# Order on ScalarE and VectorE in a routed expert kernel: casts and conversions keep their place, evictions and router steps rank higher

## The chip, the cores and the metric

The kernel runs on one core of one Trainium2 chip. The metric is the device time of one execution in microseconds (us). Its engines, each with an instruction order of its own, are TensorE (PE for its matmuls, PEld for its weight loads), VectorE (DVE), ScalarE (ACT), GpSimd (POOL) and SyncE (SP), which issues most DMAs.

## What is computed

Three stages follow one another: attention with a memory term gives 2304 tokens of 512 values; a router assigns each token to one of 8 experts with 288 places each, strictly in the order of the scores, and each expert is a pair of matrices with a relu between; a last pair of matrices has a gate between.

```python
a = softmax(causal(q @ k.T / 8));  x = g * mem_out + (1 - g) * (a @ v)     # 4 x 8 heads, 576 x 64
logits = x @ w_gate                                                        # 2304 x 8
for idx in np.argsort(-logits.flatten()):                                  # best pair first
    tok, e = idx // 8, idx % 8
    if assigned[tok] >= 0 or counts[e] >= 288: continue
    assigned[tok] = e; counts[e] += 1
y[mask_e] = np.maximum(x[mask_e] @ w1[e], 0) @ w2[e]                       # 512 -> 1024 -> 512
h = y @ w_in                                                               # 512 -> 2048, w_in is float64
out = (h * np.tanh(np.log1p(np.exp(h)))) @ w_out                           # 2048 -> 512, float64 weights
```

## The kernel before

**Stages.** `attention` fills the DRAM tensor xd (tokens) and the tile L (scores). Then `moe` does all the rest, one expert of 288 tokens at a time. Every product is made of three matmuls of 128 x 128 weights with 288 tokens (`mm3`, L1011), since both sides are held as a rounded part and a remainder; the second part of a tile is always the first's difference.

**The program of `moe`.** A list `plan` names the matmul items: `up` and `down` of the expert (pass 1), then the first half (pass 2) and second half (pass 3) of the gated pair. All pass 3 items come last, when nothing else is left to prepare. One item is usually 12 matmuls. Around the items run generators, called processes: the router (`routing`), loads of weights (`loads`), their casts (`splits`), conversions of the float64 weights (`conversions`), the gathers of tokens (`tokens`), the gates (`gate`) and the evictions of results (`relu`, `both`, `to_o`, `to_part`). `slot()` lets each process take one step; an item calls it about twice, and a process that yields n sits out n slots. A process has a class, which is its order within a slot: EVAC 0, ROUTE 1, GATE 1.5, TURN 2, LOAD 3, CONV 4.

**What sets the order on an engine.** TensorE and GpSimd issue in the order in which the program is written (`manual_schedule`, X["MO"]). ScalarE, VectorE and SyncE are ordered by a planner that simulates time: when an engine is free in its simulation, the ready operation with the best rank goes, and the rank is the place in the program, shifted by `tc.high_priority(offset=...)` (a positive offset is earlier). `tc.issue_after(ins)` adds an order edge: what the block writes on that instruction's engine is issued behind it. On the chip the order found is fixed; an operation whose input is late holds up all that stand behind it on its engine.

**Weights of the experts.** Of each expert 16 tiles are used in pass 1, 128 in all. `loads` (L921) brings one into one of five raw buffers (RAWB), once the router knows the expert (L908 reads its number). `splits` waits until LD slots after the load, then casts it on ScalarE (L942), writes its negative (L944), and lets a DMA of GpSimd add the raw value to that (L950), which leaves the remainder; once the router is done, VectorE subtracts instead (L953). Seven results are held (WFB). A raw buffer is free when the accumulation has read it. The casts have rank -400.

**Conversions.** Sixteen tiles of w_in and w_out are converted from float64 during `moe`: the load (L766, L769) and the store (L796) are issued by GpSimd; between them stand the mask (L779, VectorE), the scaling (L780, ScalarE) and five VectorE operations (L782 to L793). Sixteen others are converted during attention with SyncE as the queue. Pass 3 reads the results (`raw<-w`).

**Router.** `Router.phase` finds an expert's 288 tokens: six search steps, each a compare on VectorE (cm, L710), 18 small matmuls (L715), two short VectorE steps (ge L725, ind L727), one matmul (L730); then counts (L608, bt L634, L637) and the tokens' places (ohp L671, gc L665, L676, idx L681).

**Evictions and gates.** `relu` writes act (ScalarE L1052, VectorE L1054). `both` writes xt and y (L1002, L1004). `gate` takes sigmoid, copy, arctan and sine on ScalarE (L1076 to L1085; sines in groups of four) and four VectorE operations (L1089 to L1092).

Of the kernel before, what the change touches and what calls it, by code (L numbers as in the profile page):

```python
# [11 lines left out]
AF = mybir.ActivationFunctionType  # L12
OP = mybir.AluOpType
# [9 lines left out]
LA, LC, LD, AHEAD = 3, 0, 2, 6  # L23
# [10 lines left out]
def attention(tc, ctx, q, k, v, M_prev, z_prev, beta, w_gate, xd, L, side=None):  # L34
# [250 lines left out]
    def stage_a(u, i):  # L285
# [34 lines left out]
        if hs is None:  # L320
            nc.vector.tensor_reduce(nm, sb[:, :, 0:w], axis=AX.X, op=OP.max, negate=True)
        else:
            nc.vector.tensor_reduce(nm[:, hs:hs + 1], vw[hs][:, 0:w], axis=AX.X, op=OP.max, negate=True)  # L323
        for h in heads:
# [50 lines left out]
    def stage_d(u, i):  # L375
# [21 lines left out]
        if hp == NP - 1:  # L397
# [3 lines left out]
            nc.vector.tensor_reduce(L[d0:d0 + n, j, :], xa[d0:d0 + n, :, D:W].rearrange("p h e -> p e h"),  # L401
                                    axis=AX.X, op=OP.add)

# [141 lines left out]
class Router:  # L545
# [18 lines left out]
    def wait(self, i):  # L564
        return WAIT[2 if self.done <= self.cur + X["AH"] else self.busy][i]

# [7 lines left out]
    def phase(self, k):  # L574
# [5 lines left out]
        with self.after():  # L580
            nc.vector.tensor_reduce(m, L, axis=AX.X, op=OP.max)

# [6 lines left out]
        mx = rp.tile([128, NJ], F32, name="mx")  # L589
        nc.vector.tensor_reduce(mx, w, axis=AX.X, op=OP.max)  # L590
        oh = rp.tile([128, NJ, E], BF, name="oh")
# [158 lines left out]
LEAST, MOST = (struct.unpack("f", struct.pack("i", e << 20))[0] for e in (896, 1151))  # L750


def converter(tc, w_in, w_out):


    nc = tc.nc
    U16 = dt.uint16
    w32 = nc.dram_tensor("w32", [2, 16, 128, 512], F32, kind="Internal").ap()
    whl = nc.dram_tensor("whl", [2, 8, 128, 2, 512], F32, kind="Internal").ap()

    def convert(a, f, cv, raw, parts=None, eng=nc.gpsimd, queue=nc.sync):


        def load():
            if a == 0:
                queue.dma_start(raw.bitcast(U16).rearrange("p (a f) w -> p a (f w)", a=4),  # L766
                                w_in.bitcast(U16)[:, f * 512:(f + 1) * 512].rearrange("(a p) f -> p a f", p=128))
            else:
                queue.dma_start(raw.bitcast(U16).rearrange("p f w -> p (f w)"),  # L769
                                w_out.bitcast(U16)[f * 128:(f + 1) * 128, :])  # L770

        load()
        yield 10
        hi = raw[:, :, 1]
        t = cv.tile([128, 512], I32, name="cvt")
        e = cv.tile([128, 512], U16, name="cve")
        r = cv.tile([128, 512], F32, name="cvr")

        nc.vector.tensor_scalar(t, hi, 0x7FFFFFFF, None, op0=OP.bitwise_and)  # L779
        nc.scalar.activation(r, raw.bitcast(U16)[:, :, 1], AF.Copy, scale=2.0 ** -36)  # L780
        yield
        nc.vector.tensor_scalar(t.bitcast(F32), t.bitcast(F32), LEAST, MOST, op0=OP.max, op1=OP.min)  # L782
        yield

        nc.vector.tensor_scalar(t, t, 5, 2, op0=OP.logical_shift_left, op1=OP.logical_shift_right)
        nc.vector.scalar_tensor_tensor(t, hi, -0x40000000, t, op0=OP.bitwise_and, op1=OP.bitwise_or)
        yield

        nc.vector.tensor_scalar(e, t.bitcast(U16).rearrange("p (f w) -> p f w", w=2)[:, :, 1], 0xFF80, None,
                                op0=OP.bitwise_and)  # L790
        eng.tensor_mul(r, r, e.bitcast(BF))
        yield
        eng.tensor_add(r, r, t.bitcast(F32))  # L793
        if parts is None:
            yield 4
            queue.dma_start(w32[a, f], r)  # L796
            return
        yield
        parts = parts()
        nc.scalar.copy(parts[:, 0], r)  # L800
        nc.gpsimd.tensor_sub(parts[:, 1], r, parts[:, 0])
        nc.sync.dma_start(whl[a, f], parts.bitcast(F32))

    return convert, w32, whl


def moe(tc, ctx, C, xd, L, w1, w2, w32, whl, convert, out):
    nc = tc.nc
# [30 lines left out]
    def slot():  # L839
        for p in list(procs):  # L840
            if p[0] == hold[0]:
                continue
            p[1] -= 1
            if p[1] <= 0:
                try:
                    p[1] = next(p[2]) or 1
                except StopIteration:
                    procs.remove(p)

    def until(cond):  # L850
        while not cond():
            slot()

    EVAC, GATE, ROUTE, TURN, LOAD, CONV = X["CL"]


    def woven(ups, downs, rate):
# [76 lines left out]
    def splits():  # L934
        for c, n, key in order:
            while not flight or flight[0][4] + X["LD"] > count[0] or n - used[c] >= cap[c]:
                yield 1
            t = flight[0][3]
            dst = (fp if c == "wf" else wp).tile([128, 2, 512], F32R, name=c, bufs=cap[c])

            with tc.high_priority(offset=-400):
                nc.scalar.copy(dst[:, 0], t)  # L942
                if R.done < E:
                    nc.scalar.activation(dst[:, 1], t, AF.Copy, scale=-1.0)  # L944
            yield 1
            if R.done < E:

                while turned[0] < -1:
                    yield 1
                nc.gpsimd.dma_start(dst[:, 1].bitcast(F32), t, accum_op=OP.add)  # L950
            else:

                nc.vector.tensor_sub(dst[:, 1], t, dst[:, 0])  # L953
            flight.pop(0)
            ready[c, key] = dst
            yield 1
# [57 lines left out]
    def up(w, x, then):  # L1014

        p = hbank()
        for d in range(ND):
            mm3(p[:, 0:CAP], w, d, lambda b, d=d: x[:, b, d, :], d == 0, d == ND - 1)
            if d == 1:
                slot()  # L1020
        h = Act(fp.tile([128, 2, CAP], F32R, name="act", bufs=X["ACTB"]))
        spawn(then(h, p), GATE if then is gate else EVAC)
        return h
# [92 lines left out]
    spawn(routing(), ROUTE)  # L1116
    spawn(loads(), LOAD)
    spawn(splits(), LOAD)
    spawn(conversions(), CONV)
    for k in range(E):  # L1120
# [85 lines left out]
    for u, c, k, f in plan:  # L1206
# [26 lines left out]
    until(lambda: len(scat) == G * E)  # L1233


X = {"MO": ("PE", "Pool"), "P": 4, "P0": 4, "L1": 2, "RX": 0, "XB": 2, "LAG": 6, "TW": 18, "TS": 2, "LD": 6,
     "LG": 2, "RAWB": 5, "WFB": 7, "ACTB": 12, "GB": 7, "NG": 4, "CL": (0, 1.5, 1, 2, 3, 4), "C0": 2,
     "CW": 4, "FW": 3, "FE": 4, "AH": 2}


def program(tc, q, k, v, M_prev, z_prev, beta, w_gate, w1, w2, w_in, w_out, out):
# [54 lines left out]
```

## Time and profile before

| | us |
|---|---|
| median of three runs | 1127.38 (1124.45 to 1130.71) |
| the profiled execution | 1125.07 |
| its span, first to last instruction | 1123.2 |
| busy in the span: PE, PEld | 1009.8, 932.5 |
| busy in the span: ACT, DVE, POOL | 681.1, 652.2, 343.7 |

The profile is one execution, taken by the hardware. A line of a timeline has the start in us from the span's beginning, the duration, the engine, the line of the code, the operation, the tiles (out<-in), their shapes, the count, and in brackets how long the engine had been idle and what ended that. SPq and POOLq are the sequencers of SyncE and GpSimd. "PEclk" is the granted clock of TensorE as a share of 2.4 GHz. A wait for several things is put down to the one that came last.

### The profile page before, as it was taken

The page shows a single profiled execution, that of the slowest core. Times are in us where ns is not written, and L with a number is a line of the kernel's source. Part 1 is how long each engine was busy: PE and PEld are TensorE (multiplying, and loading weights), DVE is VectorE, ACT ScalarE, POOL GpSimd, SP SyncE. Part 2 cuts the span into 40 slices and gives each one's busy share as a digit, 9 for nine tenths or more (in the row PEclk, how much of TensorE's full clock was granted, in tenths as well). Part 3 has the DMA queues.
Part 4 walks back from the last instruction along what each step waited for, and adds up shares of the span by engine and source line. Part 5 has one row for each costly group of instructions (what it writes and reads, how often), then busy time and mean ns, then how long its engine had stood idle before and what let it go on. Part 6 is the DMA issues. An engine that isn't in the chain of part 4 may idle for free. (4 is left out here: it accounts for less than half of the span.)

```text
span 1123.2 us, 22421 instructions
## 1 busy us (share of the span) xinstructions
PE 1009.8 (90%) x8088; PEld 932.5 (83%) x8088; DVE 652.2 (58%) x1986; ACT 681.1 (61%) x1632; POOL 343.7 (31%) x468
## 2 busy tenths in 40 slices
PE   5999899999837879889789999799999999999995
PEld 4778778788726868779679888799999999999995
DVE  7877777876663565576476585566443533333332
ACT  5677676767404483564465655647483986666662
POOL 5677566674204131403304333220000001111112
PEclk9999899999957988899899999999999999999998
DMA  7899969896199685937929948755435412222201
GB/s 179 212 231 242 230 183 231 215 239 158 42 347 197 149 218 134 237 99 169 250 79 219 249 135 207 197 156 165 137 119 164 157 73 85 86 85 85 75 22 43
DMA packets 177488, 182.61 MB, mean 163 GB/s; under 512 B 90912, under 2 KB 131904, under 8 KB 175328
## 3 DMA queue, kind: packets, MB, share of 16 engines
q1 hardware_dynamic: 157152, 134.59, 41.6%
q0 software_dynamic: 20224, 46.58, 19.3%
q8 instruction: 64, 1.05, 0.4%
q14 instruction: 48, 0.39, 0.1%
HBM read 97.17 MB, written 36.18 MB: 119 GB/s over the span
## 5 line engine op out<-in xcount | busy, mean ns | idle before, releaser
L1011 PE MATMUL acc<-act,wb 128*128 128x288 f32 x1536 | 234.8, 303 | 3.1 <-ACT o L1153 1.4
L1011 PEld LDWEIGHTS acc<-act,wb 128*128 128x128 f32 x1536 | 216.5, 193 | 5.3 <-DVE act L1092 2.2
L950 POOL DMA_DIRECT2D wf<-raw x93 | 83.6, 967 | 254.9 <-ACT wf L944 184.6
L1089 DVE TENSOR_TENSOR H<-H,U 128x288 f32<-128x288 f32 x128 | 56.8, 455 | 172.3 <-ACT U L1085 172.3
L942 ACT CAST wf<-raw 128x512 fp32r<-128x512 f32 x128 | 78.7, 617 | 95.3 <-DMA raw<-moe_w 75.8
L1011 PE MATMUL h<-xt,wf 128*128 128x288 f32 x768 | 125.3, 309 | 5.4 <-DVE xt L1004 3.6
L1011 PE MATMUL h<-y,wa 128*128 128x288 f32 x768 | 119.7, 310 | 5.8 <-ACT y L1002 3.7
L1178 POOL DMA_INDIRECT out<-xg,idx x24 | 24.3, 1011 | 326.7 <-ACT xg L1175 326.1
L1011 PE MATMUL acc<-act,wf 128*128 128x288 f32 x768 | 121.1, 308 | 3.1 <-ACT act L1052 3.1
L1011 PEld LDWEIGHTS h<-xt,wf 128*128 128x128 f32 x768 | 110.5, 196 | 10.7 <-DVE xt L1004 4.6
L1011 PEld LDWEIGHTS h<-y,wa 128*128 128x128 f32 x768 | 109.5, 197 | 11.4 <-issue 3.9
L1011 PEld LDWEIGHTS acc<-act,wf 128*128 128x128 f32 x768 | 109.5, 196 | 5.3 <-ACT act L1052 3.2
L1011 PE MATMUL h<-xt,wa 128*128 128x288 f32 x768 | 113.1, 296 | 0.0
L1011 PEld LDWEIGHTS h<-xt,wa 128*128 128x128 f32 x768 | 105.2, 188 | 0.0
L1076 ACT ACTIVATE U<-h 128x288 f32<-128x288 f32 x128 | 53.1, 415 | 84.0 <-PE h L1011 83.1
L342 ACT COPY T<-pt 128x512 f32<-128x512 f32 (+3 forms) x128 | 57.7, 455 | 63.5 <-PE pt L341 63.0
L325 ACT ACTIVATE P<-s,nm 128x576 f32<-128x576 f32 (+4 forms) x160 | 84.2, 535 | 6.7 <-DVE nm L323 5.9
L1052 ACT ACTIVATE act<-h 128x288 fp32r<-128x288 f32 x64 | 25.9, 405 | 91.5 <-PE h L1011 91.3
L341 PE MATMUL pt<-ident,P 128*128 128x128 f32 x400 | 71.0, 285 | 0.5 <-DVE T L342 0.3
L367 PE MATMUL o<-T,vm 128*64 128x128 f32 x640 | 64.2, 288 | 0.0
L1054 DVE SCALAR_TENSOR_TENSOR act<-h,act 128x288 fp32r<-128x288 f32 x64 | 29.1, 454 | 60.2 <-ACT act L1052 59.9
L309 PE MATMUL s<-k,q 128*128 128x288 f32 (+3 forms) x192 | 60.0, 349 | 0.3 <-ACT P L325 0.2
(237 smaller groups left out, 2060.7 us busy)
## 6 DMA issues: line engine op xcount, KB each, us to landing
raw<-moe_w SPq DMA_DIRECT2D x128, 256.0 KB, 4.0
wf<-raw POOLq DMA_DIRECT2D x93, 256.0 KB, 4.9
k<-kh SPq DMA_DIRECT2D x60, 160.0 KB, 3.8
yd<-y SPq DMA_DIRECT2D x8, 1152.0 KB, 5.7
xt<-yd SPq DMA_DIRECT2D x8, 1152.0 KB, 5.7
whl<-parts SPq DMA_DIRECT2D x16, 512.0 KB, 5.4
part<-o SPq DMA_DIRECT2D x8, 576.0 KB, 3.4
wf<-part SPq DMA_DIRECT2D x16, 288.0 KB, 3.2
```

The source lines that it names most:

```text
L309: nc.tensor.matmul(vw[h][:, a:e], q1[:, h, r], k1[:, h, kb[h] + a:kb[h] + e], start=True, stop=False, skip_group_check=True)
L325: nc.scalar.activation(P[:, h * w:(h + 1) * w], vw[h][:, 0:w], AF.Exp, bias=nm[:, h:h + 1], scale=1.0, accum_out=den[:, h:h + 1])
L341: nc.tensor.transpose(t[:, j * 128:(j + 1) * 128], P[:, (c + j) * 128:(c + j + 1) * 128], ident)
L342: (nc.scalar.copy if eng else nc.vector.tensor_copy)(T[:, c:c + m], t[:, 0:m * 128].rearrange("p (a b) -> p a b", b=128))
L367: nc.tensor.matmul(o[s, 0:n], vm[:, j - 1 if h else 4 - j, h, :], T[:, i + j if h else i - j, 0:n], start=False, stop=(j == i), skip_group ...
L942: nc.scalar.copy(dst[:, 0], t)
L950: nc.gpsimd.dma_start(dst[:, 1].bitcast(F32), t, accum_op=OP.add)
L1011: nc.tensor.matmul(p, w[:, a, c * 128:(c + 1) * 128], x(b), start=first and i == 0, stop=last and i == 2)
L1052: nc.scalar.activation(h.t[:, 0], p[:, 0:CAP], AF.Relu)
L1054: nc.vector.scalar_tensor_tensor(h.t[:, 1], p[:, 0:CAP], 0.0, h.t[:, 0], op0=OP.max, op1=OP.subtract)
L1076: s = nc.scalar.activation(U, p[:, 0:CAP], AF.Sigmoid, scale=-1.0)
L1089: nc.vector.tensor_mul(H, H, U)
```

## The change

A helper `placed(tc, eng)` gives an order edge behind the last instruction written so far on an engine. The casts of weights use it (L942, L944), and so do a conversion's mask and scaling where its queue is GpSimd's. There the step after the load comes 14 slots later in place of 10. Each step of a process is written under a rank shift by class: +300 for evictions and router, -600 for conversions, 0 for others; the casts keep -400. LD goes from 6 to 8 and the pause between conversions, CW, from 4 to 2.

```diff
+def placed(tc, eng):
+
+    return tc.issue_after(next(i for i in reversed(tc.nc.cur_bb.bb.instructions) if i.engine == eng.engine))
...
         load()
-        yield 10
+        yield 10 if queue is nc.sync else 14
...
-        nc.vector.tensor_scalar(t, hi, 0x7FFFFFFF, None, op0=OP.bitwise_and)
-        nc.scalar.activation(r, raw.bitcast(U16)[:, :, 1], AF.Copy, scale=2.0 ** -36)
+        with nullcontext() if queue is nc.sync else placed(tc, nc.vector):
+            nc.vector.tensor_scalar(t, hi, 0x7FFFFFFF, None, op0=OP.bitwise_and)
+        with nullcontext() if queue is nc.sync else placed(tc, nc.scalar):
+            nc.scalar.activation(r, raw.bitcast(U16)[:, :, 1], AF.Copy, scale=2.0 ** -36)
...
-                    p[1] = next(p[2]) or 1
+                    with tc.high_priority(offset=AHEAD.get(p[0], 0)):
+                        p[1] = next(p[2]) or 1
...
+    AHEAD = {EVAC: X["PE"], ROUTE: X["PR"], CONV: -X["PC"]}
...
-            with tc.high_priority(offset=-400):
+            with placed(tc, nc.scalar), tc.high_priority(offset=-400):
...
-X = {"MO": ("PE", "Pool"), "P": 4, "P0": 4, "L1": 2, "RX": 0, "XB": 2, "LAG": 6, "TW": 18, "TS": 2, "LD": 6,
+X = {"MO": ("PE", "Pool"), "P": 4, "P0": 4, "L1": 2, "RX": 0, "XB": 2, "LAG": 6, "TW": 18, "TS": 2, "LD": 8,
      "LG": 2, "RAWB": 5, "WFB": 7, "ACTB": 12, "GB": 7, "NG": 4, "CL": (0, 1.5, 1, 2, 3, 4), "C0": 2,
-     "CW": 4, "FW": 3, "FE": 4, "AH": 2}
+     "CW": 2, "FW": 3, "FE": 4, "AH": 2, "PE": 300, "PR": 300, "PC": 600}
```

## Rows read from the trace of the kernel before

**Rows 1.** The page's head and part 1: busy us, share of the span, instructions.
```profile
span 1123.2 us, 22421 instructions
...
PE 1009.8 (90%) x8088; PEld 932.5 (83%) x8088; DVE 652.2 (58%) x1986; ACT 681.1 (61%) x1632; POOL 343.7 (31%) x468
```

**Rows 2.** Windows by stage: length, each engine's busy us, clock, DMA share, GB/s.
```profile
344.00:756.00 412.00, 360.07 (x2973) 337.04 (x2974) 247.09 (x861) 230.89 (x488) 124.04 (x141) 0.93 0.73 181
756.00:1100.00 344.00, 341.52 (x2566) 339.81 (x2566) 144.54 (x367) 235.18 (x505) 21.97 (x40) 1.00 0.32 103
```

**Rows 3.** Windows at clock 0.50 behind gaps of A (4), B (4), C (3): sums.
```profile
sum 23.89, PE 16.68 PEld 15.71 DVE 13.95 ACT 18.67 POOL 14.81; mean PE 4.17 PEld 3.93 DVE 3.49 ACT 4.67 POOL 3.70
...
sum 13.64, PE 13.18 PEld 12.26 DVE 7.46 ACT 6.58 POOL 3.00; mean PE 3.29 PEld 3.06 DVE 1.86 ACT 1.64 POOL 0.75
...
sum 17.06, PE 16.23 PEld 14.40 DVE 16.14 ACT 5.18 POOL 2.37; mean PE 5.41 PEld 4.80 DVE 5.38 ACT 1.73 POOL 0.79
```

**Rows 4.** PE's waits, 344 to 756: waiter, releaser, total us, times, longest us.
```profile
PE rt L715 <- DVE cm L710: 11.8, 4, 7.9
PE rt L730 <- DVE ind L727: 7.4, 4, 3.6
PE rt L637 <- DVE bt L634: 7.2, 2, 5.2
...
PE h L1011 <- ACT y L1002: 3.7, 1, 3.7
PE h L1011 <- DVE xt L1004: 3.6, 2, 3.0
PE acc L1011 <- ACT act L1052: 3.1, 1, 3.1
PE rt L715 <- DVE oh L592: 2.3, 1, 2.3
...
PE h L1011 <- ACT xt L1002: 1.7, 1, 1.7
```

**Rows 5.** ACT's waits, 344 to 756.
```profile
ACT wf L942 <- DMA raw<-moe_w: 41.6, 22, 8.3
```

**Rows 6.** Timeline around 550: a cast on ACT, and PE's end of waiting.
```profile
547.97 0.62 ACT L942 CAST wf<-raw 128x512 fp32r<-128x512 f32 x1 [8.33 <-DMA raw<-moe_w]
...
552.27 0.64 PE L715 MATMUL rt<-oh,cm 128*32 128x8 bf16 x18 [7.90 <-DVE cm L710]
```

**Rows 7.** Timeline of DVE, 694 to 698: conversion steps between router steps.
```profile
695.51 0.41 DVE L785 TENSOR_SCALAR cvt<-cvt 128x512 int32<-128x512 int32 x1
...
696.36 0.68 DVE L786 SCALAR_TENSOR_TENSOR cvt<-raw,cvt 128x512 int32<-128x512 int32 x1
696.96 0.44 DVE L634 TENSOR_REDUCE bt<-q 128x36 bf16<-128x288 bf16 x1
```

**Rows 8.** Timeline around 498: the gate's sines on ACT and the copies of xt.
```profile
496.56 1.81 ACT L1085 ACTIVATE U<-U,half_pi 128x288 f32<-128x288 f32 x4
...
498.28 0.97 ACT L1002 CAST xt<-h 128x288 fp32r<-128x288 f32 x3
```

**Rows 9.** Timeline of SP, 340 to 372: loads of the first expert's weights.
```profile
344.05 24.24 SPq L921 DMA_DIRECT2D raw<-moe_w  x11
```

**Rows 10.** Chain that ended last: start, us, one item of 12 matmuls at full clock.
```profile
1093.36 1.60 PE h L1011 x12
```

**Rows 11.** Instructions of L950 (accumulation): duration ns min/median/max, first and last start.
```profile
L950 POOL DMA_DIRECT2D wf<-raw x93: 841/857/2279, 340.2 to 742.0; - x93
...
DMA to landing us min/median/max: 3.3/4.9/7.8
```

**Rows 12.** Instructions of L921 (loads of weights), in the same form.
```profile
L921 SPq DMA_DIRECT2D raw<-w x16: 319/320/332, 845.6 to 897.4; - x16
...
DMA to landing us min/median/max: 2.4/3.8/8.0
```

**Rows 13.** Instructions of L769 (conversion's load of w_out), in the same form.
```profile
L769 POOL DMA_DIRECT2D raw<-moe_w_out x8: 554/857/1597, 409.4 to 747.7; - x8
```

## What the change will do to the time

> **What bounds the kernel now.** First the page's head: one core, a span of 1123.2 us, TensorE busy 90% of it [rows 1]. An average of 90% says little, so next the busy time by stage [rows 2]. Attention ends at 307, the router's first pass at 344. From 344 to 756 the experts are chosen and their weights prepared: TensorE is busy 360 of 412 us at a mean clock of 0.93. From 756 to 1100 it is busy 341.5 of 344 us at full clock: nothing is to be had there. The last 23 us are transposes and scatters; these, attention and the first pass the change hardly touches. So the question is what the change does to the 52 us in which TensorE stands still between 344 and 756, and to the clock there.
>
> Third view: TensorE's waits in that stretch [rows 4]. Its order is written out by hand, so a late operand of the next matmul stops everything behind it. The waits look scattered; following each back along the engine that released it gives three classes, 40.8 us of the 52.
> - A, a weight cast at the head of ScalarE. At 547.97 a cast starts after 8.33 us of waiting for its load; behind it stand the output copies (L1002), behind their subtraction on VectorE a compare of the router (cm), and TensorE starts again at 552.27 [rows 6]. The longest waits for cm, for ind, for y and for act are of this kind: 7.9 + 3.6 + 3.7 + 3.1 = 18.3 us. ScalarE waits 41.6 us for such loads in all [rows 5].
> - B, a conversion on VectorE. Between the router's short steps, which need each other, lie the conversion's long ones: L785 at 695.51, L786 at 696.36 (0.68 us), and only then bt, for which TensorE waits [rows 7]. The rest of the cm row (11.8 - 7.9 = 3.9) and the bt row (7.2) are 11.1 us.
> - C, the gate's operations ahead of an expert's tokens or a router step. At 496.56 four sines run in one go, and the copies of xt come after them [rows 8]. The rest of the ind row (7.4 - 3.6 = 3.8), the oh row (2.3) and the two xt rows (3.6 + 1.7) are 11.4 us.
>
> After each long gap the granted clock is 0.50 (1.2 GHz in place of 2.4) for some microseconds. In the stretches at 0.50 that follow the gaps of A, B and C, TensorE was busy 16.68, 13.18 and 16.23 us [rows 3]; at full clock the same work takes half, so they cost 8.3, 6.6 and 8.1 us more. What each class holds is then A 26.6, B 17.7, C 19.5 us, together 63.8.
>
> **The casts: placed, and two slots later.** Every cast gets an order edge behind the last ScalarE instruction written before it. It can no longer stand ahead of a relu or an output copy that the program has first. It costs no instruction. It does not shorten a load, and it leaves later work behind the cast. Can the weights stand it? A full-speed stretch uses one per 1.60 us (12 matmuls [rows 10]) and the program holds 7 (WFB), so a cast may start 11.2 us ahead of its use. Two casts at 0.62 us [rows 6] and the accumulating DMA, 0.86 us to issue and 4.9 to landing [rows 11], take 7.0; that leaves 4.2 us of cover. LD from 6 to 8 takes two slots. A conversion of 22 slots takes 24.2 us (seven steps of two between 409.4 and 747.7 [rows 13]), so a slot is 1.1 us, and two are 2.2: hidden, and if the cover were gone, 2.2 us for each stretch of one expert's weights. What stays is that loads are late: in the first expert 11 issues take 24.24 us, 2.4 us a weight [rows 9], half again the 1.60 that TensorE needs, because a raw buffer comes free only when the accumulation has landed. ScalarE will still wait; only what stands behind the wait changes. I take half of A, 13.3 us; the ends are 0 and 26.6.
>
> The Trainium skill (Trainium Kernel Development and Optimization, Key Constraints) speaks against this part: DMAs issued from SP, ACT and POOL share the same 16 engines and interleave. By that rule the loads are as late as before whatever ScalarE does first, A gives nothing, and the sum below is 10.7 us instead of 24; the DMA share of the stretch, 0.73 [rows 2], neither shows nor excludes it.
>
> **Conversions: first steps placed, load to first step 14 slots for 10, and 600 lower.** The mask (VectorE) and the scaling (ScalarE) can't come ahead of what the program has before them, and the four slots give the load 4.4 us more; its landing is not in these rows, but a weight load takes 2.4 to 8.0 us [rows 12]. So waits at the head of VectorE should go. The lower rank does less than it seems: rank decides only between operations that are ready, and in rows 7 the conversion's step fits in where the next router step is not ready yet. I take 0.4 of B, 7.1 us; ends 0 and 17.7. One conversion now lasts 14 + 4 + 4 + 2 = 24 slots for 22, so sixteen end 16 x 2 x 1.1 = 35 us later. The last load is issued at 747.7; nothing reads the results before 845.6 [rows 12, 13], so some 60 us are left for the last conversion itself and as cover, less what the rest gains.
>
> POOL is the queue past which this moves: the store of a conversion and its next load stand in POOL's fixed order between accumulations and gathers. If the last step comes later than the store's place, POOL waits, and the next weights with it. Bounds: 0, and 15 stores times some 1.3 us of delayed steps (L785 and L786 lengths, 0.41 + 0.68, and a little waiting) less nothing for cover, 20 us. The 4.2 us of cover are nearer; I take 2.
>
> **Evictions and router steps 300 higher.** Relu, copies of xt, y and o and all router steps now win over the gate's when both are ready; nothing is added. The four sines are ready together, so the copies of xt can now pass. A running operation is not stopped, so some remains: 0.6 of C, 11.7 us; ends 0 and 19.5. What is passed is the gate, whose results feed the second matmuls. Ten groups of four gates lie in the stretch; one long step on VectorE (0.68 us, as L786 in rows 7) ahead of each is 6.8 us, none is 0: I take 3. For weights that come late in dense places I take 3 more, with 0 and 5 x 2.2 = 11 as ends.
>
> **Sum.** Back: 13.3 + 7.1 + 11.7 = 32.1. Given up: 2 + 3 + 3 = 8. Net 24. The profiled execution took 1125.07 us (span 1123.2 and 1.9 around it): 1101. The median of the runs shown is 2.3 above it, so 1127.38 - 24 = 1103.
>
> **The rivals.**
> - Slower: the weights bind. For: 2.4 us a weight against 1.60, and casts that now keep behind work which waits for TensorE. Against: no row of that view, shown in rows 4 or not, has TensorE wait for a weight, and 4.2 us of cover. Price: 93 of the 128 weights go through the accumulation [rows 11]; if half of them run at 2.4, 46 x 0.8 = 37 us, and five new gaps with a half-clock stretch after each cost about 5 x 1.7 = 8; less the gains of B and C after their costs (18.8 - 8 = 11) it is +34, 1161. It decides once casts slip by over 4.2 us; a slip just past it gives 1133 to 1161.
> - No change: the edge binds only to the one instruction before, the order on ScalarE stays in effect, and gate waits replace what C gives: 1122 to 1133. For: ScalarE is busy 231 of 412 us [rows 2], so ready casts go at once. Against: the edge counts even then.
> - The loads decide alone: A gives 0, and the rest 24 - 13.3 = 10.7: 1117. The waits for loads merely move to other places in ScalarE's order. This is what the rule of the Trainium skill named under the casts would give.
> - All three classes go: 63.8 less a few, 1064 to 1080. Against: rows 7, where rank can't help.
>
> **How the numbers follow.** Forecast (1085 to 1112, at 1103) 0.42; loads alone (1117) 0.12; everything goes 0.13; no change 0.16; weights bind 0.17. Half a per cent, about what a measurement of this kernel can tell from no change, is 5.6 us: faster 0.42 + 0.12 + 0.13 = 0.67, same 0.16, slower 0.17. The range 1074 to 1136 leaves out about half of "everything goes" and most of "weights bind", 0.2. It holds both signs; the forecast's own range is 1085 to 1112.
>
> **What would show it.** Right: between 344 and about 735 the idle time of TensorE falls from 52 to about 35 us, the waits for y, act and ind that began with a cast are shorter than 2 us, fewer stretches stand at 0.50; 0 to 344 and the full-speed stage keep their lengths. The bt row (B) should shrink least. The wait of ScalarE for loads (41.6) may stay: if it falls to a few microseconds, A was undersized. Wrong: TensorE waiting directly for wf, a new row of POOL waiting for the conversion's last step, longer waits for the gate's act, or a first pass of other length.

## The result and the profile after

The kernel after takes 1117.40 us (median of 7 runs, 1112.46 to 1120.69), the kernel before beside it 1127.86 us (7 runs). The ratio is 0.9905, with a 95% interval of 0.9876 to 0.9934: 10.5 us less, where 24 were forecast. Once more on another chip the change came to 0.9909 (0.9877 to 0.9942). So it is faster by about one per cent, less than half of what the sum said.

The profiled execution of after is its fastest, 1112.46 us, beside 1125.07 before; its difference, 12.6 us, is a little larger than that of the medians. The line numbers from L942 on have moved by ten (cast L952, accumulation L960, matmuls L1021), the conversion's by six or seven (L779 is L785).

The head of the page after, to be held against [rows 1]: all engines do the same work in a shorter span.

```profile
span 1110.7 us, 22438 instructions
...
PE 1006.2 (91%) x8088; PEld 930.1 (84%) x8088; DVE 655.5 (59%) x1986; ACT 680.6 (61%) x1632; POOL 343.9 (31%) x468
```

The windows by stage after, in the form of [rows 2]. Expert 6 begins its first product at 741.5 here and at 753.4 before, so the same middle stage ends some 12 us earlier, and the window is cut to fit.

```profile
344.00:744.00 400.00, 357.68 (x2980) 335.75 (x2981) 244.35 (x851) 235.63 (x498) 123.44 (x139) 0.93 0.75 184
744.00:1088.00 344.00, 342.64 (x2572) 340.69 (x2570) 150.29 (x378) 234.83 (x503) 24.38 (x44) 1.00 0.34 107
```

TensorE stood still for 51.9 us in the middle stage before and stands still for 42.3 now; the full-speed stage keeps its length, as expected, and the clock of the middle stage is still 0.93. TensorE's waits after, 344 to 745, in the columns of [rows 4]:

```profile
PE rt L676 <- DVE ohp L671: 10.6, 3, 6.4
PE rt L730 <- DVE ind L727: 8.3, 6, 3.7
PE h L1005 <- DMA xg<-xd,idx: 8.3, 4, 4.5
PE rt L637 <- DVE bt L634: 3.9, 4, 2.0
PE h L1021 <- DVE xt L1014: 3.4, 2, 2.8
PE rt L715 <- DVE oh L592: 3.4, 1, 3.4
PE rt L715 <- DVE cm L710: 2.4, 4, 1.3
```

The cm row has fallen from 11.8 to 2.4 us, bt from 7.2 to 3.9, and the rows that waited for ScalarE's y and act (3.7 and 3.1) are gone. Two rows are new at the top: L676, which needs ohp, and the transposes of an expert's gathered tokens. The other queues, same stretch:

```profile
ACT wf L952 <- DMA raw<-moe_w: 31.8, 23, 4.8
...
POOL w L803 <- DVE cvr L800: 21.5, 1, 21.5
POOL w L803 <- DVE X L718: 11.6, 1, 11.6
```

ScalarE still waits 31.8 us for loads at the casts, before 41.6 [rows 5], and POOL now waits for a conversion's last steps.

Where the time went is best seen expert by expert. The table gives the start of the first matmul of expert k's first product, us from the start of the profiled execution, found by counting the matmuls of the plan:

| | k=0 | k=2 | k=3 | k=5 | k=7 | last item |
|---|---|---|---|---|---|---|
| before | 344.4 | 500.2 | 578.9 | 682.6 | 807.4 | 1107.3 |
| after | 346.8 | 489.2 | 561.9 | 669.5 | 794.1 | 1094.9 |
| difference | +2.4 | -11.0 | -17.0 | -13.1 | -13.3 | -12.4 |

After starts expert 0 2.4 us later, though the prediction said that the change hardly touches the first pass; it gains 19 up to expert 3 and gives back 4 between experts 3 and 5. Two things were therefore to be explained: why the gain stops at expert 3, and whether the first pass lost time.

### The profile page after: what moved, and what is told of

Same layout as the page of the kernel before. It is cut to its first block, busy times and chain, and to the rows that moved or that the text cites. A ratio compares the mean times of both kernels' runs of the same rounds, so it can differ in the third digit from the quotient of the medians.

```text
span 1110.7 us, 22438 instructions
## 1 busy us (share of the span) xinstructions
PE 1006.2 (91%) x8088; PEld 930.1 (84%) x8088; DVE 655.5 (59%) x1986; ACT 680.6 (61%) x1632; POOL 343.9 (31%) x468
## 3 DMA queue, kind: packets, MB, share of 16 engines
q1 hardware_dynamic: 157152, 134.59, 42.3%
## 4 chain that ended last, share of the span: by engine, by line
PE 65%; DVE 10%; ACT 9%; DMA 9%; issue 3%; SPq 1%; POOL 1%; POOLq 0%; ACTq 0%; DVEq 0%
PE acc L1021 22%; PE h L1021 22%; PE o L367 4%; DMA raw<-moe_w 3%; PE pt L341 3%; DMA wf<-raw 2%; PE s L309 2%; PE o L390 2%; PE o L359 2%; PE rt L715 2%; PE s L313 2%; ACT L1095 2%; PE o L363 1%; ACT U L1095 1%; DVE H L1099 1%
## 5 line engine op out<-in xcount | busy, mean ns | idle before, releaser
L1021 PE MATMUL acc<-act,wb 128*128 128x288 f32 x1536 | 236.1, 304 | 2.3 <-DVE act L1102 2.3
L1021 PEld LDWEIGHTS acc<-act,wb 128*128 128x128 f32 x1536 | 217.5, 193 | 4.1 <-DVE act L1102 3.7
L960 POOL DMA_DIRECT2D wf<-raw x93 | 82.3, 912 | 219.4 <-ACT wf L954 122.6
L952 ACT CAST wf<-raw 128x512 fp32r<-128x512 f32 x128 | 79.1, 618 | 85.5 <-DMA raw<-moe_w 65.9
L1021 PE MATMUL h<-xt,wf 128*128 128x288 f32 x768 | 124.4, 309 | 3.4 <-DVE xt L1014 3.4
L1021 PE MATMUL acc<-act,wf 128*128 128x288 f32 x768 | 119.9, 307 | 0.0
L1021 PEld LDWEIGHTS h<-xt,wf 128*128 128x128 f32 x768 | 110.7, 197 | 9.6 <-issue 5.0
L1021 PE MATMUL h<-xt,wa 128*128 128x288 f32 x768 | 114.2, 297 | 1.3 <-DVE wa L963 1.0
L1021 PE MATMUL h<-y,wa 128*128 128x288 f32 x768 | 114.6, 302 | 0.0
L1021 PEld LDWEIGHTS acc<-act,wf 128*128 128x128 f32 x768 | 108.4, 194 | 2.0 <-issue 1.4
L1021 PEld LDWEIGHTS h<-y,wa 128*128 128x128 f32 x768 | 105.8, 191 | 3.6 <-issue 3.0
L1021 PEld LDWEIGHTS h<-xt,wa 128*128 128x128 f32 x768 | 105.3, 188 | 2.5 <-DVE wa L963 1.6
```

The source lines that it names most:

```text
L1021: nc.tensor.matmul(p, w[:, a, c * 128:(c + 1) * 128], x(b), start=first and i == 0, stop=last and i == 2)
```

## The experiments

Theory P was formed on comparing the traces: the order edges make the gain, and the rank shifts cost something. Its rival R: the rank shifts make it. The reason for P was in the order of VectorE's operations. A rank block gives the rank count back where it ends. In the change every process step is written in such a block, so steps written one after another start from the same count, and the order within the router changes: before, every phase runs ohp 0, ohp 1, gc, ohp 2; in the change ohp 0, which the first matmul of L676 needs, comes last in four of the eight phases and behind ohp 2 in six.

**The parts alone.** e1_casts has the casts' edges (the hunk of the diff at the cast) and eight slots and nothing else; e4_ranks the rank shifts alone (the hunks with AHEAD); e6_noranks all edges and spacings of the change without the shifts; e5_going the whole change with a count that goes on:

```diff
-                    with tc.high_priority(offset=AHEAD.get(p[0], 0)):
+                    with tc.high_priority(offset=AHEAD.get(p[0], 0) - grown[0]):
+                        n = len(tc.nc.cur_bb.bb.instructions)
                         p[1] = next(p[2]) or 1
+                    grown[0] += len(tc.nc.cur_bb.bb.instructions) - n
```

Expected of e1_casts:

> The casts' part alone: the order edge on the casts of weights and LD 8; no rank shifts, conversions as before. Theory P (the edges made the gain, the ranks as written cost): ratio to before 0.987 to 0.993, some 11 us faster; the gaps of TensorE behind casts (18.3 us before: the longest waits for cm, ind, y and act) fall below 8 us. Theory R (the raised evictions and router steps made the gain, and the edges only move ScalarE's waits for loads): ratio 0.998 to 1.003, and the gaps behind casts stay above 12 us.

Expected of e4_ranks:

> The rank shifts alone (+300 evictions and router, -600 conversions, every step of a process written under its shift); no edges, LD 6, conversions' waits as before. Theory P: ratio 0.997 to 1.006, since the rank counter does not go on inside a step's shift, so that steps written one after another share ranks and the router's own operations change places (the first ohp part, which the first matmul of the token places needs, comes last); the wait of L676 for ohp is 5 us or more. Theory R: ratio 0.988 to 0.994.

Expected of e5_going:

> The whole change, but with a rank counter that goes on: each step's rank is its place in the program less its shift, as before the change. Theory P: the router's operations keep their order (first ohp part first); the first pass is 2.4 us shorter again than with the change, the wait of L676 falls from 10.6 to about 5 us, and the ratio to before is 0.980 to 0.987, 5 to 9 us faster than the change. Theory R: what counts is who is ahead of whom between classes, not the order within one: same as the change, 0.989 to 0.992.

Expected of e6_noranks:

> The change without rank shifts: edges on casts and on the conversions' first steps, LD 8, 14 slots, CW 2. Theory P: 0.983 to 0.990, faster than the change by 0 to 7 us, since the edges' gain stays and the ranks' cost goes. Theory R: 0.997 to 1.003.

Measured against 1131.61 us of before on that chip:

| | median us | ratio (95%) |
|---|---|---|
| e1_casts | 1121.65 | 0.9892 (0.9843 to 0.9941) |
| e4_ranks | 1140.33 | 1.0073 (1.0045 to 1.0101) |
| e5_going | 1110.53 | 0.9795 (0.9740 to 0.9849) |
| e6_noranks | 1110.76 | 0.9797 (0.9739 to 0.9855) |

R falls: the shifts alone make the kernel slower, and without them the change is twice as good. With a count that goes on the shifts cost nothing and give nothing.

The traces bear out less of P than the times. e5_going and e6_noranks came out a little faster than P's ranges. The row of L676 is 9.2 us in e5_going, where P wanted about 5, and in e4_ranks its wait for ohp is 4.0, where P wanted 5 or more; what has grown there is the cm row, from 11.8 to 23.4 us. And e1_casts shows its gain in the time alone. Its one trace is its slowest execution (1125.81 us); TensorE stands still for 52.0 us between 344 and 745 in it, before for 51.9, and where P wanted the gaps behind casts under 8 us in all, the chain of [rows 6] is still there. Timelines of ScalarE and of TensorE, e1_casts:

```profile
543.75 0.62 ACT L947 CAST wf<-raw 128x512 fp32r<-128x512 f32 x1 [9.31 <-DMA raw<-moe_w]
...
545.35 0.38 ACT L1007 CAST y<-acc 128x288 fp32r<-128x288 f32 x1
```

```profile
548.04 0.64 PE L715 MATMUL rt<-oh,cm 128*32 128x8 bf16 x18 [8.12 <-DVE cm L710]
```

The edge binds a cast behind the one ScalarE instruction written last before it, and this y still comes behind this cast. Where the 10 us of e1_casts lie stays open.

**Is it the order of the router's steps?** Theory O says yes; S, that the shifts cost by something else; N, that they cost nothing and the sets differ by chance. Four kernels on one chip: the change itself (e8_change), the edges alone again (e6_again), the conversions' part alone (e2_conv), and the change with all its shifts, in which the router's steps are tied in the order of before (e10_tied). Shown are the ties of ohp and gc, the line of gc having moved from its old place; the two halves of cm are tied in the same way:

```diff
-                nc.vector.tensor_tensor(op_[:, s], bj(pl[:, s], GP),
-                                        C["i96"][:, None, :].to_broadcast([128, 6, GP]), op=OP.is_equal)
+                with self.tc.issue_after(x.ins) if c else nullcontext():
+                    x = nc.vector.tensor_tensor(op_[:, s], bj(pl[:, s], GP),
+                                                C["i96"][:, None, :].to_broadcast([128, 6, GP]), op=OP.is_equal)
+            if c == 1:
+                with self.tc.issue_after(x.ins):
+                    x = nc.vector.tensor_tensor(gc, gk[:, :, :, None].to_broadcast([128, NJ, G, 2]),
+                                                C["codes"][:, :, None, :].to_broadcast([128, NJ, G, 2]), op=OP.mult)
```

Expected of e8_change:

> The change itself once more, beside the others of this set. Theory O (the rank shifts as written turn round the router's pairs on VectorE, ohp and cm, and that is what they cost): ratio to the kernel before 0.988 to 0.992, row of matmuls of L676 that wait for ohp about 10 us. Theory S (the shifts cost by something else, such as evictions that push casts back): the same ratio. Theory N (the shifts cost nothing, and the 1 per cent between the change and the edges alone was only the difference between two sets of runs): 0.978 to 0.983.

Expected of e6_again:

> The edges of casts and conversions, eight slots, no rank shifts, once more beside the change. All theories: 0.978 to 0.983. O and S want it 0.7 to 1.2 per cent under the change of this set, N within 0.3 per cent of it.

Expected of e10_tied:

> The change whole, with its rank shifts, and five edges more in the router: the two halves of cm and the steps ohp 0, ohp 1, gc, ohp 2 are tied in the order in which the kernel before runs them. O: 0.979 to 0.984, the first pass as long as before, the row of L676 under ohp 4 to 7 us. S: 0.988 to 0.992 as the change. N: 0.978 to 0.983.

Measured: e8_change 1120.04 us, 0.9909 (0.9877 to 0.9942); e6_again 1110.85, 0.9829 (0.9796 to 0.9863); e10_tied 1111.43, 0.9834 (0.9801 to 0.9866). Tying these few steps, with every shift left in place, gives back 8.6 us, all that lies between the change and the edges alone. O holds against S and N in the time.

The traces show how. Timeline of VectorE after, about 720 (start, us, engine, line, operation):

```profile
718.78 1.42 DVE L671 TENSOR_TENSOR ohp<-pl,i 128x576 bf16<-128x576 bf16 x2
720.12 0.26 DVE L665 TENSOR_TENSOR gc<-gk,codes 128x108 bf16<-128x108 f32 x1
720.30 0.75 DVE L671 TENSOR_TENSOR ohp<-pl,i 128x576 bf16<-128x576 bf16 x1
```

and of TensorE there:

```profile
721.11 0.43 PE L676 MATMUL rt<-gc,ohp 128*96 128x6 bf16 x6 [2.37 <-DVE ohp L671]
```

The same place in e10_tied, VectorE:

```profile
715.53 1.42 DVE L670 TENSOR_TENSOR ohp<-pl,i 128x576 bf16<-128x576 bf16 x2
716.86 0.27 DVE L674 TENSOR_TENSOR gc<-gk,codes 128x108 bf16<-128x108 f32 x1
717.05 0.75 DVE L670 TENSOR_TENSOR ohp<-pl,i 128x576 bf16<-128x576 bf16 x1
```

and TensorE:

```profile
717.18 0.39 PE L679 MATMUL rt<-gc,ohp 128*96 128x6 bf16 x6 [1.71 <-DVE gc L674]
```

The operations on VectorE are alike within 0.01 us. But in the change the first matmul needs the third ohp and starts 0.81 us after that began; in e10_tied it starts 0.13 us after. In the change a wait of the same kind stands at 454 (1.86 us), which e10_tied has with 1.19. In the first pass it is visible too. TensorE after, then in e10_tied:

```profile
314.33 1.12 PE L715 MATMUL rt<-oh,cm 128*64 128x8 bf16 x18 [2.43 <-DVE cm L710]
...
334.85 1.60 PE L676 MATMUL rt<-gc,ohp 128*96 128x6 bf16 x18 [3.57 <-DVE ohp L671]
```

```profile
314.04 1.31 PE L719 MATMUL rt<-oh,cm 128*64 128x8 bf16 x18 [1.75 <-DVE cm L714]
...
334.17 1.52 PE L679 MATMUL rt<-gc,ohp 128*96 128x6 bf16 x18 [2.99 <-DVE gc L674]
```

The start of expert 0 tells less: it is at 346.8 and 349.4 in the two profiled executions of the change and at 344.8 to 346.1 in e5, e6 (twice) and e10, but at 347.0 and 347.1 in e11_ld6 and e12_ld11 below, which have no shifts. The four waits named carry some 2.6 us of the 8.6. The row of L676 in e10_tied, at 9.6 us for gc, is hardly shorter than the 10.6 of after and missed what O expected of it (4 to 7): its longest wait, 6.1 us, follows a cast that waited 4.74 us for its load, and in after one that waited 4.80. The rest I see only in the clock. The windows of e8_change and e10_tied, two executions of one set whose spans differ by 8.7 us:

```profile
344.00:745.00 401.00, 354.50 (x2965) 331.69 (x2965) 242.69 (x847) 233.23 (x495) 125.75 (x142) 0.93 0.75 183
```

```profile
344.00:745.00 401.00, 357.49 (x3029) 336.03 (x3028) 250.16 (x862) 238.41 (x505) 123.49 (x140) 0.95 0.75 186
```

At the lower level, 0.50, are 53.9 us of this stretch in e8_change and 40.8 in e10_tied, and TensorE was busy in 43.5 and 33.5 of them. At full clock that work takes half as long, so the difference is worth some 5 us, by estimate. Why the clock differs so much, these rows don't show.

**The shifts with a good count, and the number of slots.** e14_goingalone has the shifts on a count that goes on, and no edges. e11_ld6, e12_ld11 and e13_ld14 are e6_noranks with another distance from load to cast, for e11_ld6:

```diff
-X = {"MO": ("PE", "Pool"), "P": 4, "P0": 4, "L1": 2, "RX": 0, "XB": 2, "LAG": 6, "TW": 18, "TS": 2, "LD": 8,
+X = {"MO": ("PE", "Pool"), "P": 4, "P0": 4, "L1": 2, "RX": 0, "XB": 2, "LAG": 6, "TW": 18, "TS": 2, "LD": 6,
```

Expected of e14_goingalone:

> The rank shifts alone (300, 300, 600) with a counter that goes on, so that the router keeps its own order; no edges, six slots. The prediction's theory (the ranks bring xt, the router's steps and evictions ahead of gate and conversions): 0.985 to 0.992, waits for cm down from 11.8 us, for xt and y from 7.3. Theory P (the shifts move nothing that TensorE waits for): 0.997 to 1.003.

Expected of e11_ld6:

> Both sets of edges, no rank shifts, but the casts six slots behind their loads, as in the kernel before, and not eight. If the slots are what keeps the edges from costing (theory D, the cover of the prediction): 0.985 to 0.995, ScalarE's waits for loads at the casts 45 to 60 us against 31.8 in the change. If the edge alone does it (theory E): 0.978 to 0.984.

Expected of e12_ld11:

> Both sets of edges, no rank shifts, eleven slots. Theory D: ScalarE's waits for loads at the casts fall from some 32 us to under 15, and with them the waits for ind and ohp that a waiting cast makes (3.99 and 4.95 us with eight): 0.970 to 0.978. Rival W (the weights then come late, since a cast three slots later gives its weight 3.3 us later): 0.984 to 0.995, waits of TensorE for a weight's accumulation appear.

Expected of e13_ld14:

> Both sets of edges, no rank shifts, fourteen slots. With 5 raw buffers and a load each two slots or more, a cast 14 slots behind holds the buffers longer. Theory D: as eleven slots or 2 to 4 us better. Rival W: 0.99 to 1.02, TensorE waiting for weights by several us for each expert.

Measured against 1131.24 us: e14_goingalone 1131.10, 1.0010 (0.9981 to 1.0038); e11_ld6 1110.89, 0.9823 (0.9778 to 0.9867); e12_ld11 1108.79, 0.9803 (0.9759 to 0.9847); e13_ld14 1131.34, 1.0001 (0.9976 to 1.0026).

The shifts as they were meant shorten nothing that TensorE waits for. Its waits in e14_goingalone, 344 to 745, with y and xt where they were in [rows 4] and cm longer:

```profile
PE rt L715 <- DVE cm L710: 17.3, 6, 8.1
...
PE h L1022 <- DVE xt L1015: 4.4, 3, 3.0
PE h L1022 <- ACT y L1013: 3.5, 1, 3.5
```

In the change itself the copies of xt still come behind the gate's sines, as in [rows 8]. ScalarE after:

```profile
485.78 1.81 ACT L1095 ACTIVATE U<-U,half_pi 128x288 f32<-128x288 f32 x4
487.50 0.97 ACT L1012 CAST xt<-h 128x288 fp32r<-128x288 f32 x3
```

Six slots or eight make no difference, so theory D falls for these: with six, ScalarE waits 29.3 us for loads at the casts, where D had 45 to 60. With eleven the middle stage is another one, but the time is not. Its windows, the wait of ScalarE for loads at the casts in 344 to 745, and TensorE's waits after 745, e12_ld11:

```profile
344.00:745.00 401.00, 368.82 (x3081) 345.91 (x3082) 254.32 (x872) 240.48 (x512) 120.04 (x140) 0.94 0.77 189
756.00:1100.00 344.00, 334.00 (x2475) 330.90 (x2473) 139.43 (x362) 223.62 (x476) 27.14 (x50) 0.99 0.30 94
```

```profile
ACT wf L949 <- DMA raw<-moe_w: 7.9, 6, 2.6
```

```profile
PE h L1018 <- ACT wa L949: 3.4, 3, 2.1
PE h L1018 <- DVE wa L960: 2.5, 4, 1.6
```

ScalarE waits 7.9 us for loads instead of some 33, TensorE is busy 368.8 of the 401 us (355.2 in e6_again), and expert 7 starts 22.0 us ahead of before, in e6_again 15.0. Then the last stage's weights come late, with some microseconds at half clock, and the last item is only 14.3 us ahead, no more than in e6_again. Its ratio lies between what D and what W expected. With fourteen slots this is worse, and the experts' own weights are late too: TensorE waits 9.8 us for accumulations. That is the prediction's slower rival, met three to six slots further out; here W is right.

**Which half of the conversions' part?** e2_conv, in the set above, had it alone, edges and spacing (14 slots, CW 2):

> The conversions' edges alone (with 14 slots and CW 2), casts and slots of the loads as before, no shifts. If the two sets of edges add up (casts alone 0.989, both 0.980): 0.989 to 0.993, waits for cm after step 1 of the search down from 11.8 to about 3 us, casts' waits as before. Rival (the conversions' edges only tell once the casts no longer hold the evictions): 0.996 to 1.002.

It measured 1117.69 us, 0.9884 (0.9851 to 0.9917): 13.2 us, a little more than the first of the two expectations has, where the prediction gave the part 7.1. And it takes away the long wait for cm that e1_casts keeps, though no cast has an edge and ScalarE waits 50.4 us for their loads:

```profile
PE rt L715 <- DVE cm L710: 1.7, 2, 1.1
```

The next kernels take it apart. e15_slots has the spacing alone, e16_convedge both edges alone, e17_dveedge VectorE's edge alone; e19_bothedges and e20_castslots have the edges, and the spacing, each beside the casts' edges with eight slots. Against before, the spacing and VectorE's edge are:

```diff
-        yield 10
+        yield 10 if queue is nc.sync else 14
...
-     "CW": 4, "FW": 3, "FE": 4, "AH": 2}
+     "CW": 2, "FW": 3, "FE": 4, "AH": 2}
```

```diff
-        nc.vector.tensor_scalar(t, hi, 0x7FFFFFFF, None, op0=OP.bitwise_and)
+        with nullcontext() if queue is nc.sync else placed(tc, nc.vector):
+            nc.vector.tensor_scalar(t, hi, 0x7FFFFFFF, None, op0=OP.bitwise_and)
```

The last kernel of this set goes on from eleven slots. e18_split is e12_ld11, so eleven slots for the experts' weights, with six for the last stage's:

```diff
-            while not flight or flight[0][4] + X["LD"] > count[0] or n - used[c] >= cap[c]:
+            while not flight or flight[0][4] + (X["LD"] if c == "wf" else 6) > count[0] or n - used[c] >= cap[c]:
```

Expected of e15_slots:

> Of the conversions' part only the spacing: 14 slots between a conversion's load and its first step, CW 2; no edges at all, no shifts. If the spacing gives what the conversions' part gave (theory S): 0.985 to 0.992, waits of ScalarE and VectorE for the conversions' loads down from 19.8 and 22 us to under 6. If the edges give it (theory E): 0.996 to 1.003, those waits over 12 us each.

Expected of e16_convedge:

> Of the conversions' part only the edges, on VectorE's and ScalarE's first steps, with 10 slots and CW 4 as before. Theory E: 0.985 to 0.992. Theory S: 0.996 to 1.003, since ten slots are 11 us and the loads of the conversions took longer than that where VectorE waited for them.

Expected of e17_dveedge:

> Of the conversions' part only the edge on VectorE's first step; ScalarE's step stands where the order of ranks puts it, 10 slots, CW 4. If VectorE's wait is the one that matters, as the prediction has it (class B, waits for cm): as with both edges, 0.985 to 0.992. If ScalarE's step counts as much: 0.993 to 0.998.

Expected of e18_split:

> Both sets of edges, no shifts, 11 slots for the experts' weights and 6 for those of the last stage. With eleven slots throughout, the waits over 1 us between 344 and 745 came to 15.5 us against 35, and the last stage lost 6 us to late weights at 758 to 890. If that is all that took the gain back: 1099 to 1105 us, ratio 0.972 to 0.977. Rival (the gain in the middle is a matter of the clock and comes back as slow stretches): 1107 to 1111.

Expected of e19_bothedges:

> Casts' edges (eight slots) and conversions' edges, but the conversions spaced as before (10 slots, CW 4); no shifts. Without the casts' edges the conversions' edges at this spacing gave nothing (1.0007). If that was because the casts then held the evictions in their place (theory M): with the casts' edges they give, 0.978 to 0.985. If the spacing is needed in itself (theory S): 0.987 to 0.992, as the casts' edges alone.

Expected of e20_castslots:

> Casts' edges (eight slots) and the conversions' spacing of 14 slots and CW 2, without the conversions' edges; no shifts. Without the casts' edges the spacing alone cost 1 per cent. Theory M: the spacing by itself moves no first step, so 0.987 to 0.995, near the casts alone or a little worse, with VectorE and ScalarE still waiting over 20 us for conversions' loads. Theory S: 0.978 to 0.985.

(The traces have the waits over 1 us that the expectation of e18_split compares at 18.5 and 39.1 us.) Measured, with before at 1131.17 us for the first four and 1128.67 for the last two:

| | median us | ratio (95%) |
|---|---|---|
| e15_slots | 1141.54 | 1.0103 (1.0073 to 1.0133) |
| e16_convedge | 1132.17 | 1.0007 (0.9983 to 1.0030) |
| e17_dveedge | 1137.53 | 1.0066 (1.0040 to 1.0092) |
| e18_split | 1101.01 | 0.9754 (0.9723 to 0.9784) |
| e19_bothedges | 1128.08 | 0.9997 (0.9971 to 1.0024) |
| e20_castslots | 1138.25 | 1.0064 (1.0038 to 1.0090) |

Neither half gives anything, alone or beside the casts' edges, whose own 10 us it even takes away; the spacing without the edges stands 0.6 to 1.0 per cent above before; and both together give more than one. No theory on record had that. One reason was not tested: for each of these kernels the planner orders ScalarE, VectorE and SyncE anew, and no run keeps the rest of the order as it was, so a per cent either way can come from places that the edit doesn't name. Part of it can be read. In e15_slots the first steps still wait at the heads of their engines, since nothing binds them to their later place. ScalarE's waits and VectorE's, 344 to 745:

```profile
ACT cvr L780 <- DMA raw<-moe_w_in: 18.0, 5, 6.4
...
DVE cvt L779 <- DMA raw<-moe_w_in: 16.2, 5, 5.7
```

In e19_bothedges these waits are nearly gone (2.4 us on each engine), yet expert 3, 13.9 us ahead of before, is followed by losses that leave expert 7 at +1.1. They begin with a cast again. Timeline of ScalarE:

```profile
537.99 0.62 ACT L949 CAST wf<-raw 128x512 fp32r<-128x512 f32 x1 [8.01 <-DMA raw<-moe_w]
...
539.04 0.38 ACT L1009 CAST y<-acc 128x288 fp32r<-128x288 f32 x1
```

and of TensorE:

```profile
541.05 0.64 PE L715 MATMUL rt<-oh,cm 128*32 128x8 bf16 x18 [6.19 <-DVE cm L710]
```

This is the chain of [rows 6] once more, with an edge on the cast. At the same place after, the cast waits 4.28 us for its load, ahead of a relu:

```profile
526.92 0.62 ACT L952 CAST wf<-raw 128x512 fp32r<-128x512 f32 x1 [4.28 <-DMA raw<-moe_w]
...
527.98 0.39 ACT L1062 ACTIVATE act<-h 128x288 fp32r<-128x288 f32 x1
```

After has the shifts too; e6_again, which differs from e19_bothedges in the spacing alone, has TensorE wait 3.3 us at this place. So the spacing of the conversions seems to decide, among other things, how late a cast's load is and what stands behind it there; which of the loads a conversion's transfer meets, the rows do not settle. If this is all, e19_bothedges with eleven slots should come down to e18_split; that was not tried.

e18_split settles what took back the gain of eleven slots. Its windows, TensorE's waits (344 to 745) and ScalarE's:

```profile
344.00:745.00 401.00, 369.14 (x3108) 346.44 (x3108) 255.30 (x874) 241.41 (x514) 118.64 (x139) 0.95 0.78 191
756.00:1085.00 329.00, 326.73 (x2452) 324.75 (x2450) 134.87 (x349) 217.16 (x465) 24.74 (x47) 1.00 0.31 97
```

```profile
PE rt L715 <- DVE cm L710: 5.8, 7, 2.6
PE rt L676 <- DVE gc L665: 5.6, 3, 3.0
PE h L1002 <- DMA xg<-xd,idx: 4.7, 3, 2.5
PE acc L1018 <- DMA wf<-raw: 3.7, 5, 1.3
```

```profile
ACT wf L949 <- DMA raw<-moe_w: 12.7, 10, 4.0
```

No wait of TensorE is over 3.0 us, the lead over before is 23.6 us at expert 3 and 28.7 at expert 7, and the last item keeps 27.9 of it: with later casts the gain no longer stops at expert 3. At 1101.01 us this version beats both kernels: 30 us less than before, and 19 less than the change in its set, where before measured nearly the same.

## Why the prediction was wrong, and where it was right

The direction was right, the size was not: 10.5 us came, 24 were forecast. The step that failed is the term for the ranks. It put down 11.7 us back, less 3 for the gate; the runs show 0.1 us with a good count and a loss of 8.6 as the change is written. Taken by its own steps:

- **The casts, 13.3 us forecast.** Alone, with eight slots, they gave 10.0 us (0.9892). The number was near; that it came about as the step says is not shown, and in part it did not. Of class A the longest row, 7.9 us for cm, stands at 8.1 in e1_casts and the one for act at 3.0; gone are y (3.7) and the longest for ind (3.6), while the wait for an expert's gathered tokens grew from 0.8 to 7.3. The 7.9 us went with the conversions' part. The edge still leaves relu or y behind a late cast in places, as at 526.92. The sign set down for it, that waits for y, act and ind beginning with a cast would be under 2 us, came for y and act and not for ind: 3.68 us at 526 begin so, and 6.41 for ohp at 688. The sentence "if it falls to a few microseconds, A was undersized" is borne out in direction: from e11_ld6 to e18_split that wait falls from 29.3 to 12.7 us, and the time by another 10.
- **LD, two slots of cover.** Said to be hidden, and so it was: six, eight and eleven slots give 1110.9, 1110.8 and 1108.8 us. The reckoned cover of 4.2 us, four slots, ends between eleven slots, where weights are late mainly in the last stage, and fourteen, where all is lost.
- **The conversions, 7.1 us forecast.** The part gave 13.2 us alone and 10.9 beside the casts (1121.65 to 1110.76). Rows of class B shrank more than said: cm to 2.4 us, and bt, which "should shrink least", from 7.2 to 3.9; and the part took away a row of class A besides. The term was undersized, and its parts were not understood: they do not add up, and why they work only together stays partly open.
- **POOL, 2 us forecast.** The row of POOL waiting for the conversion's last steps appeared, 21.5 and 11.6 us, and was set down as a sign against the prediction. It costs nothing that shows: e18_split, the fastest of all, has 50.7 us of it over 307 to 756.
- **The ranks, 11.7 us back, 3 for the gate.** This is the step that failed, and by most: 20.3 us lie between the 11.7 and the loss of 8.6. The sentence "evictions and router steps now win over the gate's when both are ready" was never decisive: with a good count the shifts give 0.1 us (e14_goingalone), and beside the edges 0.2 (e5_going against e6_noranks). The xt row stands at 3.4 us, for the copies still come behind the sines. The sentence that failed worst is "nothing is added": as written, the shifts turn round the router's own steps and cost 8.6 us. The prediction looked at whom a shift passes, and not at what it does to the order within the class that is shifted.
- **The sum.** By measured terms it is 10.0 + 10.9 + 0 - 8.6 = 12.3 us; 10.5 was measured. Against the 24 forecast, the ranks' gain that did not come (11.7), their cost (8.6) and the casts (3.3) are on one side, the conversions (3.8) and the 8 us of given-up time that did not show on the other.

The time fell on the number of the rival "the loads decide alone", 1117, but not by its mechanism. It had the casts giving nothing and the ranks giving all of their share; the runs show the reverse. The rule that stood beside it, from the Trainium skill (Trainium Kernel Development and Optimization, Key Constraints), that transfers from the queues of SP, ACT and POOL run on the same 16 engines and interleave, is not contradicted: the casts waited for loads after the change too, 31.8 us. What does not follow is that ScalarE's order and the time of the casts are worth nothing: e1_casts is 10 us faster by an edge and two slots (the two slots were not taken out alone there; beside both sets of edges they are worth 0.1), and e12_ld11 shows the waits nearly gone with a DMA share of 0.77 against 0.75.

## What to carry to other kernels

An order written by priorities has two readers: the classes that pass each other, and the steps within one class; after any edit to the priorities, compare the order of each engine's operations before asking what the ranks are worth. Where an in-order engine waits at a load, moving the wait gives something, and starting the consumer later gives more on top (10 us from e11_ld6 to e18_split), until the consumer's own deadline is met; and that deadline differs by stage, so one constant for all stages (eleven slots here) can win 7 us up to the last expert and lose them again in the last stage. Parts of an edit to such a schedule need not add up: measure each alone and beside the others, and look whether the waits that a part was meant for are the ones that went.

## What was not expected of the hardware

The wait on POOL for a conversion's store, up to 21.5 us in one piece, with the next weights' accumulations in the same queue behind it, shows in no wait of TensorE after the change: no row there is for an accumulation. With eleven slots there is one, of 3.6 and 3.7 us (e12_ld11 and e18_split); whether POOL's wait makes it is not shown. And the middle stage's granted clock does not follow the sum of TensorE's waits: after and e10_tied stand still for 42.3 and 43.5 us between 344 and 745, at a clock of 0.93 and 0.95, with 58 and 41 us at the lower level, 1.2 GHz.
